# A rational activation behind an attention: a constant added by accumulating DMAs, Horner's form in more half units, and a new order of all steps

## The chip, the cores and the metric

One core of a Trainium2 chip runs the whole kernel in one launch. The metric is the device time in microseconds. A core has the engines TensorE (PE, with PEld for its weight loads), VectorE (DVE), ScalarE (ACT) and GpSimd (POOL), which run their own queues of instructions in order, and SyncE (SP), which here issues DMAs. Engines wait for each other through semaphores.

## The reference

Attention without a softmax, on features of degree two, and behind it one dense layer with a rational activation:

```python
def phi(x):                       # S1, S2: 8 x 32; 64 features
    a = einsum('rd,bhsd->bhsr', S1, x); b = einsum('rd,bhsd->bhsr', S2, x)
    return einsum('bhsi,bhsj->bhsij', a, b).reshape(..., 64)
kv = einsum('bhsf,bhsd->bhfd', phi(k), v);  z = phi(k).sum(axis=2)
x = (phi(q) @ kv) / (phi(q) @ z + 1e-6)     # 4 batches, 4 heads, 1088 tokens, 32 wide
h = x.reshape(4352, 128) @ w_in             # to 2048 wide
P = a[0] + a[1]*h + a[2]*h**2 + a[3]*h**3
Q = 1 + abs(b[0])*abs(h) + abs(b[1])*h**2
out = (P / (Q + 1e-6)) @ w_out              # 4352 x 128
```

## The kernel before

The 4352 tokens go through the dense layer in tiles: one of 256, seven of 512, and two of 256 at the end. With the 2048 rows of h on top, the work is cut into 17 *units* of 4096 columns by 128 partitions, each with two *half units* of 2048 columns; half unit n belongs to unit n // 2. A tile of 512 tokens has two units, one of 256 has one. The last unit is done partly in quarters.

One step of a unit is a word with a number and the unit behind the colon: `m1:5` is step m, part 1, of unit 5. A step that is done for both halves at once ("wide") is done at part 1.

- `h` (PE): four matrix products in f32 that make 1024 columns of h in PSUM. `e` (ACT): copies them to `hh` in bf16.
- `u` (DVE): |h|, by masking the sign. `ln` (ACT): the square that makes Q but for a factor and a constant. `ex` (ACT): the reciprocal of its root. The square of that, `r` = 1/Q, is made by `rd` on DVE, or by `ra` on ACT where `R_ON_ACT` has a 1.
- `pd` (DVE; `pa` on ACT for the last): p = a3*h + a2.
- `s` (DVE): s = h*r.
- `m` (DVE): the first product g. `x` (DVE): the second one, in place.
- `G` (PE): adds w_out times r, s and g to the tile's output in PSUM. There are three scaled copies of w_out (a0, a1 and 1 times a common factor), so that the output is a0*r + a1*s + g.
- `st`: DVE transposes a finished tile into `out_sb`, SP (at the end ACT too) stores it.

A half unit has one of two forms. In the plain form m makes g = h*s and x makes g = g*p; then r, s and g are multiplied by their copies of w_out, twelve matmuls where the tile has 512 tokens. In *Horner's form* m makes g = h*p, a step `v` adds a1 (a `tensor_scalar` on DVE over 128x2048), x makes g = g*s, and only r and g are multiplied: the four matmuls with s are left out. The tuple `HORNER` names the half units in that form. `WIDE_S`, `WIDE_M`, `WIDE_X` and `WIDE_P` name the units whose step is one instruction over 4096 columns, `SPLIT_A` those whose u is done by halves. r, s and g stand in rings of four half units, p in one of two.

The attention is in steps for keys (`kt`, `ks`, `kc`, `kf`, `kp`, `kk`) and for thirteen blocks of queries (`qt` transpose, `qs` sketch, `qc` copy, `qf` features, `qp` products, `qd`, `qi`, `qx` quotient, `qb` and `qk` back into xT). From block 3 on, qc sends the sketches to DRAM and reads them back spread over the partitions: SP issues four writes, then three reads, and qf on DVE waits for these. `lk`, `lq`, `lv`, `lw`, `lx` are loads on SP; k, q and v have one buffer each, so a load waits until the one before is used. `wo` scales w_out, `ba` makes |b| on ACT and the constants of Q on POOL, `bi` and `rg` finish them.

The order of all engines' queues is one hand-written list, `ORDER`; each engine takes its own steps from it in that order. So an engine waits whenever its next step isn't ready, and nothing overtakes.

At the end stands a branch: `special` is 1 if the constants b don't fit the fast form, and then the general kernel runs. The step `fl` loads the flag into a register on every engine; `hi` marks the branch's likely way.

Of the kernel before, what the change touches and what calls it, by code (L numbers as in the profile page):

```python
# [29 lines left out]
e1:1 h1:2 v1:0 u0:1 qf:3 qc:4 ln0:0 kc1:2 e3:1 ex0:0 kp1:1 qp:3 pd1:1 kf1:2 h3:2 ln0:1 s1:0 e1:2 rd0:0 qd:3 qi:3 G3:0  # L30
h0:2 ex0:1 e3:2 kk:1 e0:2 G0:0 x1:0 G5:0 qx:3 u1:1 qf:4 qs:5 qp:4 s0:0 u0:2 ln1:1 h2:2 lq:2 lk:3 qc:5 qd:4 qi:4 ex1:1
qt:7 qx:4 qb:3 qk:3 qb:4 lv:2 qk:4 x0:0 rd0:1 m1:1 ks0:2 qs:7 e2:2 u1:2 ln0:2 rd1:1 h2:3 v0:1 h0:3 e2:3 h1:3 v1:1
kc0:2 kf0:2 kt1:3 s1:1 ex0:2 qt:9 qf:5 e0:3 e1:3 kt0:3 ln1:2 G3:1 G2:0 h3:3 x1:1 h0:4 qc:7 e3:3 h3:4 ra0:2 st:0 qp:5
ex1:2 qd:5 qi:5 e0:4 ra1:2 kp1:2 s0:2 qx:5 G0:2 qs:6 u1:3 pd1:2 e3:4 qb:5 h1:4 qk:5 m0:2 G0:1 m1:2 h0:5 s1:2 qf:7
ln0:3 qc:6 e1:4 ln1:3 h2:4 x0:2 v1:2 G2:1 e0:5 ex1:3 qt:8 x1:2 pd1:3 h3:5 G1:2 kk:2 e2:4 ks0:3 ex0:3 qp:7 u1:4 e3:5
qs:8 ln0:4 rd0:3 rd1:3 h2:5 qd:7 e2:5 G3:2 qf:6 qc:8 s1:3 h1:5 G2:2 kc0:3 ln1:4 G5:1 kf0:3 qi:7 e1:5 lq:3 ex0:4 ex1:4
h1:6 G5:2 m1:3 h3:6 qx:7 u1:5 G3:3 ra0:4 qs:9 qp:6 x1:3 G0:3 rd1:4 G2:3 e1:6 ln0:5 st:2 pd1:4 lv:3 s1:4 h0:6 e3:6
ln1:5 qd:6 qi:6 qb:7 qf:8 G4:3 qx:6 qk:7 h2:6 m1:4 e0:6 qc:9 G0:4 ex1:5 qb:6 qk:6 qp:8 qt:10 ks1:3 h2:7 e2:6 G3:4
ex0:5 u1:6 x1:4 e2:7 h0:7 qd:8 ln1:6 G5:3 rd1:5 qi:8 h3:7 G1:4 G5:4 qt:12 G1:3 e0:7 G2:4 pd1:5 rd0:5 ex1:6 e3:7 h1:7
m1:5 kc1:3 ra1:6 qf:9 ln0:6 qx:8 e1:7 qp:9 qs:10 ex0:6 v0:5 qd:9 h1:8 s1:5 G4:4 u1:7 pd1:6 qc:10 h3:8 e1:8 st:4 qt:11  # L40
v1:5 rd0:6 qi:9 qb:8 G3:5 ln0:7 kf1:3 e3:8 ln1:7 h0:8 h2:8 x1:5 qk:8 qs:11 e0:8 ex1:7 kp1:3 s1:6 qx:9 G0:5 e2:8 G5:5
ex0:7 h2:9 kk:3 qf:10 h3:9 u1:8 qb:9 ra0:7 m0:6 G0:6 ra1:7 qs:12 m1:6 qc:11 x0:6 ln0:8 v1:6 e3:9 pd1:7 e2:9 qp:10 qk:9
qd:10 s1:7 G2:5 ln1:8 x1:6 G3:6 h0:9 qi:10 e0:9 h1:9 m1:7 ex0:8 qx:10 e1:9 pd1:8 v1:7 h1:10 u1:9 e1:10 rd0:8 ex1:8
rd1:8 G0:7 h0:10 G2:6 ln1:9 G3:7 e0:10 G1:6 ex1:9 qb:10 v0:7 h2:10 qk:10 e2:10 h3:10 s1:8 G5:6 qf:11 qp:11 ln0:9 h3:11
rd1:9 e3:10 h0:11 qd:11 ex0:9 m1:8 qi:11 e3:11 e0:11 u1:10 G3:8 G4:8 h2:11 x1:7 h1:11 x0:7 G2:7 ln1:10 qc:12 rd0:9
ln0:10 x1:8 e2:11 e1:11 G0:8 s1:9 ex1:10 ex0:10 G5:7 G1:8 h1:12 qx:11 qb:11 ra1:10 pd1:9 h0:12 qk:11 m1:9 u1:11 G0:9
x1:9 e1:12 G2:8 e0:12 h3:12 h2:12 rd0:10 qf:12 ln1:11 ln0:11 G5:9 G5:8 G1:9 s1:10 e2:12 G3:9 qp:12 ex0:11 pd1:10 e3:12
G0:10 ex1:11 m1:10 u1:12 rd0:11 h2:13 G3:10 ln1:12 ln0:12 e2:13 h3:13 qd:12 e3:13 G4:9 G2:9 rd1:11 h1:13 ex0:12 x1:10
h0:13 st:6 e1:13 s1:11 u1:13 ex1:12 pd1:11 m1:11 e0:13 G3:11 rd0:12 h2:14 ln1:13 h3:14 e2:14 G2:10 u0:13 ln0:13 G4:10
e3:14 qi:12 G1:11 x1:11 G1:10 rd1:12 qx:12 h1:14 ex1:13 st:8 s1:12 pd1:12 ex0:13 h0:14 e1:14 G0:11 qb:12 e0:14 ra0:13  # L50
rd1:13 G1:12 G5:10 G5:11 G4:11 qk:12 G3:12 h0:15 u1:14 ln0:14 m1:12 ln1:14 st:10 h1:15 x1:12 G0:12 G2:11 e0:15 h3:15
G4:12 ex1:14 e1:15 h2:15 s1:13 ex0:14 G3:13 pd1:13 m0:13 u0:15 G5:12 rd1:14 m1:13 e3:15 ln0:15 h1:16 e2:15 G4:13 G0:13
ex0:15 rd0:14 h0:16 G2:12 u1:15 ln1:15 e1:16 h2:16 G1:13 ex1:15 e0:16 x1:13 s1:14 ra0:15 G5:13 pd1:14 st:12 G2:13
G1:14 h3:16 m1:14 u0:16 x1:14 ra1:15 ln0:16 e2:16 ex0:16 e3:16 s1:15 u2:16 m1:15 G0:14 u3:16 G5:14 G1:15 G0:15 G3:14
# [66 lines left out]


def run(
# [525 lines left out]
    @skip()  # L649
    def d_v(i, h, hh):  # L650
        if horner(i, h):
            g = part_of(i, "g", h)
            nc.vector.tensor_scalar(out=g, in0=g, scalar1=a1, scalar2=None, op0=AX.add)
# [27 lines left out]
    def store(i):  # L681
        t0, tl, f0, per = units[i]
        if f0 + per < nf:
            return
# [1 line left out]
        nc.vector.transpose(out=o[:, :tl], in_=outs[t0][:, :tl])  # L686
# [106 lines left out]
    def flag():
        value.append(nc.values_load(special[0:1, :], min_val=0, max_val=1, skip_runtime_bounds_check_because="a comparison gives 0 or 1"))
# [9 lines left out]
    for step in plan.ORDER:  # L804
        name, i = step.split(":")
        i = int(i)
        if name in q_does:
            getattr(blocks[i](), q_does[name])()
        elif name in k_does:
            getattr(keys[i](), k_does[name][0])(*k_does[name][1:])  # L810
        elif name == "wo":
            w_part(i)
        elif name in loads:
            fetched[name, i] = loads[name](i)
        elif name == "tn":
            turn(i)
        elif name == "ba":
            nc.scalar.activation(out=b_abs, in_=b_sb, func=ACT.Abs)
# [49 lines left out]
```

## Time and profile before

| | us |
|---|---|
| median of three runs | 251.97 (251.5 to 252.45) |
| the profiled execution, its own time | 251.9 |
| its span, from the first to the last instruction | 250.0 |
| busy: PE, DVE, ACT, POOL | 240.5, 233.0, 227.9, 7.5 |
| HBM read and written | 16.16 MB and 3.15 MB |

The profile is of one execution. A *group* is all instructions of one line, engine, operation and shape; its row gives the count, then busy time, the mean duration in ns, and the idle time of the engine just before them with what ended it. L647 is line 647 of the listing. Instructions of one engine overlap by a little, so that a duration is somewhat more than what an instruction takes of the queue. TensorE's granted clock is 0.998 in the mean over the span.

### The profile page before, as it was taken

What the parts mean: (1) busy time and instruction counts of PE and PEld (TensorE: products, weight loads), DVE (VectorE), ACT (ScalarE), POOL (GpSimd) and SP (SyncE); (2) the same over time, 40 slices, a digit from 0 to 9 for tenths busy, and PEclk for the clock granted to TensorE, in tenths of its full rate; (3) what the DMA queues carried; (4) which work ended last, traced back from release to release, by engine and by line L of the source; (5) the groups of instructions that cost most, each with busy time, mean ns of one, the idle gap of its engine ahead of it and who ended that gap; (6) DMA issues with size and microseconds to landing.
All of it is one profiled execution on the core that took longest, in us unless ns stands there. A gap on an engine that the chain in (4) does not pass through costs nothing.

```text
span 250.0 us, 4083 instructions
## 1 busy us (share of the span) xinstructions
PE 240.5 (96%) x1585; PEld 133.8 (54%) x1585; DVE 233.0 (93%) x233; ACT 227.9 (91%) x217; POOL 7.5 (3%) x43
## 2 busy tenths in 40 slices
...
GB/s 155 257 387 89 99 121 188 134 156 78 144 27 100 28 202 138 69 45 16 148 22 77 67 3 0 16 102 3 0 42 0 40 25 22 0 37 8 0 49 42
DMA packets 30534, 19.60 MB, mean 78 GB/s; under 512 B 20400, under 2 KB 26672, under 8 KB 30512
## 3 DMA queue, kind: packets, MB, share of 16 engines
...
q8 instruction: 13, 0.21, 0.4%
q14 instruction: 9, 0.07, 0.1%
HBM read 16.16 MB, written 3.15 MB: 77 GB/s over the span
## 4 chain that ended last, share of the span: by engine, by line
PE 77%; DVE 13%; DMA 3%; issue 3%; SPq 0%; DVEq 0%
PE h_ps L519 42%; PE att_ps L677 23%; PE att_ps L428 4%; DVE g L658 4%; PE att_ps L364 4%; DVE g L647 3%; DVE s L643 2%; DMA k_sb<-in_k_dram 2%; PE att_ps L455 2%; DMA v_sb<-in_v_dram 2%; PE att_ps L473 2%; PE att_ps L323 1%; DVE p L600 1%; DVE r L630 1%; DVE out_sb L686 1%
## 5 line engine op out<-in xcount | busy, mean ns | idle before, releaser
L519 PE MATMUL h_ps<-xT,w_in_sb 128*128 128x512 f32 (+1 forms) x320 | 125.8, 532 | 0.0
L519 PEld LDWEIGHTS h_ps<-xT,w_in_sb 128*128 128x128 f32 x320 | 59.3, 190 | 44.4 <-issue 34.0
L525 ACT CAST hh<-h_ps 128x1024 bf16<-128x1024 f32 x68 | 72.2, 1086 | 2.1 <-PE h_ps L519 1.9
L613 ACT ACTIVATE ln<-u 128x2048 f32<-128x2048 bf16 (+1 forms) x35 | 67.2, 1950 | 0.0
L677 PEld LDWEIGHTS <-w_out 128*128 128x128 bf16 x432 | 41.8, 98 | 46.0 <-issue 16.5
L618 ACT ACTIVATE r<-ln 128x2048 bf16<-128x2048 f32 x22 | 44.0, 2002 | 0.0
L643 DVE TENSOR_TENSOR s<-hh,r 128x4096 bf16<-128x4096 bf16 (+2 forms) x21 | 39.2, 1872 | 0.0
L677 PE MATMUL att_ps<-r,w_out 128*128 128x512 bf16 (+1 forms) x160 | 34.8, 347 | 0.1
L677 PE MATMUL att_ps<-g,w_out 128*128 128x512 bf16 (+1 forms) x160 | 34.4, 347 | 0.0
L647 DVE TENSOR_TENSOR g<-hh,s 128x4096 bf16<-128x4096 bf16 (+2 forms) x16 | 27.8, 1744 | 0.3 <-PE att_ps L677 0.3
L658 DVE TENSOR_TENSOR g<-g,p 128x4096 bf16<-128x4096 bf16 (+2 forms) x15 | 27.7, 1849 | 0.0
L630 DVE TENSOR_TENSOR r<-r 128x2048 bf16<-128x2048 bf16 x22 | 26.5, 1217 | 0.0
L677 PE MATMUL att_ps<-s,w_out 128*128 128x512 bf16 (+1 forms) x112 | 24.5, 349 | 0.4 <-DVE s L643 0.4
L618 ACT ACTIVATE ln<-ln 128x2048 f32<-128x2048 f32 (+1 forms) x13 | 24.4, 1895 | 0.0
L624 ACT ACTIVATE r<-ln 128x2048 bf16<-128x2048 f32 (+1 forms) x13 | 23.7, 1868 | 0.0
L600 DVE TENSOR_SCALAR p<-hh,a_sb 128x4096 bf16<-128x4096 bf16 (+1 forms) x17 | 21.6, 1273 | 0.6 <-ACT hh L525 0.6
L548 DVE TENSOR_SCALAR u<-hh 128x2048 uint16<-128x2048 uint16 (+2 forms) x24 | 21.7, 905 | 0.4 <-ACT hh L525 0.4
L647 DVE TENSOR_TENSOR g<-hh,p 128x2048 bf16<-128x2048 bf16 (+1 forms) x7 | 11.6, 1663 | 0.0
L658 DVE TENSOR_TENSOR g<-g,s 128x2048 bf16<-128x2048 bf16 (+1 forms) x8 | 11.6, 1463 | 0.0
L428 PEld LDWEIGHTS att_ps<-kvz,q_pT 128*64 128x64 f32 x288 | 9.8, 137 | 3.3 <-issue 1.7
L428 PE MATMUL att_ps<-kvz,q_pT 128*64 128x66 f32 x288 | 11.1, 224 | 0.0
L364 PE MATMUL att_ps<-v_sb,k_p 128*64 128x64 f32 (+1 forms) x288 | 9.2, 222 | 1.0 <-DMA v_sb<-in_v_dram 1.0
...
## 6 DMA issues: line engine op xcount, KB each, us to landing
...
```

The costliest lines, as they stand in the source:

```text
L428: nc.tensor.matmul(self.nd[g * 64:(g + 1) * 64, o:o + 2 * KW], lhsT=self.q_p[:, c, x + g * 64:x + (g + 1) * 64], rhs=kvz[self.b % 2][:, c, ...
L519: nc.tensor.matmul(t[:, x * tl:(x + 1) * tl], lhsT=w_in_sb[:, f * 128:(f + 1) * 128], rhs=xT[:, x_at(t0):x_at(t0) + tl], start=True, stop= ...
L525: nc.scalar.copy(out=live[i]["hh"][:, part * PW:(part + 1) * PW], in_=live[i]["h", part])
L600: nc.vector.tensor_scalar(out=part_of(i, "p", h), in0=hh, scalar1=a3, scalar2=a2, op0=AX.mult, op1=AX.add)
L613: nc.scalar.activation(out=t, in_=live[i]["u"][:, span(h)], func=ACT.Square, scale=k_in_reg, bias=1.0)
L618: nc.scalar.activation(out=t if r_on_act(i, h) else part_of(i, "r", h), in_=t, func=ACT.Abs_reciprocal_sqrt, scale=k_sq_reg, bias=1.0)
L624: nc.scalar.activation(out=part_of(i, "r", h), in_=live[i]["ln", h], func=ACT.Square)
L630: nc.vector.tensor_mul(out=t, in0=t, in1=t)
L643: nc.vector.tensor_mul(out=part_of(i, "s", h), in0=hh, in1=part_of(i, "r", h))
L647: nc.vector.tensor_mul(out=part_of(i, "g", h), in0=hh, in1=part_of(i, "p" if horner(i, first(h)) else "s", h))
L658: nc.vector.tensor_mul(out=g, in0=g, in1=part_of(i, "s" if horner(i, first(h)) else "p", h))
L677: nc.tensor.matmul(outs[t0][:, :tl], lhsT=w_sb[y][:, f0 + x, :], rhs=part_of(i, key, h)[:, c:c + tl], start=done[0] == 0, stop=done[0] == ...
```

## The change

- `HORNER` has 25 half units instead of 10: 0 to 19, 22, and 24 to 27.
- In those, a1 is no longer added on DVE. A row `a1_row` (128x2048, bf16, every element a1) is made once by ACT, behind |b| in step `ba`; `v` is now a DMA issued by POOL that adds this row onto g in SBUF. x waits for it.
- `R_ON_ACT` loses half units 5 and 21, whose square goes to DVE. `SPLIT_A` is (0, 2, 3, 13, 16), `WIDE_S` gains unit 2, `WIDE_M` loses 1 and 11 and gains 2, 6 and 13, `WIDE_X` loses 4, 11 and 15 and gains 2, 6 and 7.
- The flag: `fl` loads it on SP, ACT and POOL only. A new last step `fm` copies, on POOL, first an element of the last output tile and then the flag into `late_special`, and PE and DVE load it from there.
- All steps stand in a new order. The dependences stay as they are. Among other things block 3's sketch (qs:3) comes ahead of block 2's, ln1:0 ahead of e1:0, lk:2 behind qc:3, and lv:3 behind st:4.

```diff
-    R_ON_ACT = (0, 0, 0, 0, 1, 1, 0, 0, 1, 0, 0, 0, 0, 1, 1, 1, 0, 0, 0, 0, 0, 1, 0, 0, 0, 0, 1, 0, 0, 0, 1, 1, 1, 1)
+    R_ON_ACT = (0, 0, 0, 0, 1, 0, 0, 0, 1, 0, 0, 0, 0, 1, 1, 1, 0, 0, 0, 0, 0, 0, 0, 0, 0, 0, 1, 0, 0, 0, 1, 1, 1, 1)
     ORDER = """
...
-kc2:0 qt:1 kf2:0 qc:0 kp0:0 ba:0 kp1:0 qf:0 kp2:0 qt:3 qs:1 kk:0 bi:0 qt:2 lq:1 lv:1 qc:1 qf:1 qp:0 qd:0 qs:2 qi:0
-qx:0 qb:0 wo:3 qc:2 qk:0 qf:2 wo:0 qp:1 qs:3 qp:2 qd:1 wo:5 wo:1 h2:0 qd:2 wo:4 e2:0 qi:1 h3:0 qx:1 qi:2 h0:0 wo:2
-qx:2 qb:1 rg:0 kt0:1 e3:0 e0:0 qb:2 pd1:0 qk:2 h1:0 kt1:1 u1:0 m1:0 lk:2 qk:1 e1:0 qc:3 ks0:1 ks1:1 qt:6 qt:4 h2:1
-pd0:0 u0:0 kc0:1 kc1:1 kf0:1 m0:0 kt0:2 ln1:0 h0:1 e2:1 kt1:2 ex1:0 e0:1 v0:0 rd1:0 h1:1 ks1:2 qs:4 kf1:1 h3:1 qt:5
+kc2:0 qt:1 kf2:0 qc:0 kp0:0 ba:0 kp1:0 qf:0 kp2:0 qt:3 qs:1 kk:0 bi:0 qt:2 lq:1 qc:1 qf:1 qp:0 qs:3 qs:2 qd:0 qi:0
+qx:0 qc:2 qb:0 qk:0 qp:1 lv:1 qf:2 wo:5 qd:1 wo:2 qi:1 qp:2 qc:3 wo:1 h2:0 qd:2 qx:1 wo:3 h3:0 rg:0 qb:1 wo:4 qi:2
+e2:0 qx:2 qb:2 wo:0 e3:0 h0:0 kt1:1 qk:1 kt0:1 ks1:1 qk:2 pd1:0 e0:0 ks0:1 kc1:1 u1:0 m1:0 v1:0 ln1:0 h1:0 kc0:1 kf1:1
+e1:0 h1:1 ex1:0 h2:1 kf0:1 e1:1 u0:0 pd0:0 qt:4 m0:0 rd1:0 qs:4 h0:1 e2:1 ln0:0 qt:6 s1:0 qf:3 lk:2 qc:4 e0:1 h3:1
+v0:0 x1:0 kp1:1 qp:3 h0:2 e3:1 u1:1 ex0:0 kk:1 kt0:2 qd:3 qt:5 kt1:2 ln1:1 ln0:1 G3:0 qi:3 pd1:1 e0:2 qx:3 qs:5 ks1:2
...
+h3:8 m1:5 e0:7 qf:9 kf0:3 qi:8 qc:10 x0:4 h2:8 ra1:6 v0:5 e3:8 e2:8 u1:7 ln0:7 G2:4 h1:8 rd0:6 pd1:6 qs:11 qp:9 e1:8
+ex0:7 qx:8 G0:5 st:4 h0:8 qb:8 ln1:7 v1:5 qk:8 m1:6 ex1:7 qd:9 x1:5 v1:6 lv:3 s1:6 G3:5 G0:6 qf:10 e0:8 u1:8 h3:9 e3:9
...
-G4:15 G5:15 pa2:16 pa3:16 s2:16 G6:16 hi:0 m3:16 G1:16 G4:16 G2:15 m2:16 G3:16 G7:16 x0:16 st:15 G2:16 x2:16 G5:16
-x3:16 G8:16 fl:0 st:16
+pa0:16 s3:16 s2:16 m3:16 G7:16 hi:0 pa2:16 G1:16 m2:16 x0:16 pa3:16 G1:15 G3:16 st:15 G4:16 x2:16 G2:16 G5:16 x3:16
+G8:16 fl:0 st:16 fm:0
     """.split()
-    SPLIT_A = (0, 1, 2, 13, 15, 16)
+    SPLIT_A = (0, 2, 3, 13, 16)
-    WIDE_S = (1, 3, 4, 5, 6, 7, 8, 9, 10, 11, 12, 13, 14, 15)
-    WIDE_M = (1, 3, 4, 5, 7, 8, 9, 10, 11, 12, 14, 15)
-    WIDE_X = (1, 3, 4, 5, 8, 9, 10, 11, 12, 13, 14, 15)
+    WIDE_S = (1, 2, 3, 4, 5, 6, 7, 8, 9, 10, 11, 12, 13, 14, 15)
+    WIDE_M = (2, 3, 4, 5, 6, 7, 8, 9, 10, 12, 13, 14, 15)
+    WIDE_X = (1, 2, 3, 5, 6, 7, 8, 9, 10, 12, 13, 14)
-    HORNER = (0, 1, 2, 3, 5, 10, 11, 13, 14, 15)
+    HORNER = (0, 1, 2, 3, 4, 5, 6, 7, 8, 9, 10, 11, 12, 13, 14, 15, 16, 17, 18, 19, 22, 24, 25, 26, 27)
...
+    a1_row = big.tile([128, 2048], BF, name="a1_row") if fast else None
+    late_special = consts.tile([1, 1], mybir.dt.int32, name="late_special")
...
     def d_v(i, h, hh):
         if horner(i, h):
             g = part_of(i, "g", h)
-            nc.vector.tensor_scalar(out=g, in0=g, scalar1=a1, scalar2=None, op0=AX.add)
+            if fast:
+                nc.gpsimd.dma_start(out=g, in_=a1_row, accum_op=AX.add)
+            else:
+                nc.vector.tensor_scalar(out=g, in0=g, scalar1=a1, scalar2=None, op0=AX.add)
...
         o = mid.tile([128, TC], FP, name="out_sb")
+        last_out[:] = [o]
...
     def flag():
-        value.append(nc.values_load(special[0:1, :], min_val=0, max_val=1, skip_runtime_bounds_check_because="a comparison gives 0 or 1"))
+        for e in (nc.sync, nc.scalar, nc.gpsimd):
+            e.reg_load(special_regs[e.engine], special[0:1, :])
+
+    def late_flag():
+        nc.gpsimd.tensor_copy(out=late_special, in_=last_out[0][0:1, 0:1])
+        nc.gpsimd.tensor_copy(out=late_special, in_=special[0:1, :])
+        for e in (nc.tensor, nc.vector):
+            e.reg_load(special_regs[e.engine], late_special)
+        value.append(nc.snap(special_handles, min_val=0, max_val=1))
...
             if fast:
                 fitting()
+                nc.scalar.activation(out=a1_row.rearrange("p (c x) -> p c x", c=4), in_=idle[:, None, :].to_broadcast([128, 4, 512]),
+                                     func=ACT.Identity, bias=a1, scale=1.0)
```

More of the change, by code (lines that the diff above doesn't have):

```diff
@@ L30 @@
[L30 to L54, printed above, removed]
@@ new lines @@
+e1:0 h1:1 ex1:0 h2:1 kf0:1 e1:1 u0:0 pd0:0 qt:4 m0:0 rd1:0 qs:4 h0:1 e2:1 ln0:0 qt:6 s1:0 qf:3 lk:2 qc:4 e0:1 h3:1
+v0:0 x1:0 kp1:1 qp:3 h0:2 e3:1 u1:1 ex0:0 kk:1 kt0:2 qd:3 qt:5 kt1:2 ln1:1 ln0:1 G3:0 qi:3 pd1:1 e0:2 qx:3 qs:5 ks1:2
+rd0:0 h2:2 m1:1 ex0:1 qb:3 s0:0 h1:2 kc1:2 qk:3 qf:4 m0:1 lk:3 ks0:2 lq:2 kt0:3 qc:5 qp:4 e2:2 e1:2 lv:2 h3:2 qd:4
+qi:4 u0:2 ex1:1 qx:4 v0:1 G5:0 qt:7 rd1:1 kc0:2 e3:2 u1:2 pd1:2 qb:4 kf1:2 G0:0 qk:4 ln0:2 kf0:2 rd0:1 h0:3 h1:3 x0:0
+ln1:2 e0:3 v1:1 qs:6 e1:3 qs:7 u0:3 h2:3 ex1:2 G3:1 G0:1 s1:1 qf:5 x1:1 qc:7 qt:9 h3:3 e2:3 G2:0 m1:2 ex0:2 ln0:3 qp:5
@@ new lines @@
+st:0 e3:3 ra0:2 rd1:2 qd:5 h0:4 qi:5 u1:3 qx:5 G5:1 e0:4 h1:4 qf:7 h3:4 ex0:3 e1:4 G3:2 pd1:3 qb:5 ln1:3 h2:4 qt:8
+s1:2 e3:4 qc:6 kp1:2 qk:5 v0:2 v1:2 e2:4 ex1:3 kk:2 u1:4 h0:5 rd0:3 rd1:3 ln1:4 kt1:3 x1:2 h1:5 e0:5 G2:1 G0:2 m1:3
+qp:7 ln0:4 h3:5 qf:6 e1:5 ex0:4 h2:5 e3:5 ex1:4 qs:8 lq:3 pd1:4 qp:6 s1:3 G5:2 v0:3 qd:6 G2:2 h2:6 qi:6 qc:8 qd:7
+qt:10 e2:5 qx:6 u1:5 qi:7 ra0:4 h3:6 rd1:4 ks0:3 ks1:3 qx:7 st:2 e2:6 m1:4 qb:6 ln0:5 v1:3 e3:6 s1:4 kc1:3 qb:7 ln1:5
+qk:7 h1:6 e1:6 x1:3 qk:6 h0:6 e0:6 qf:8 G3:3 qs:9 qt:11 G0:3 kc0:3 ex1:5 u1:6 h2:7 v0:4 ex0:5 pd1:5 qc:9 G0:4 rd0:5
@@ new lines @@
+ln0:9 e3:10 rd1:8 v1:7 qp:11 m1:8 G0:7 qb:9 qk:9 h0:10 qx:10 G3:7 ex0:9 e0:10 x1:7 qb:10 h2:10 qk:10 ln1:9 qd:11 G5:7
+e2:10 h2:11 v0:8 s1:8 G0:8 ex1:9 G2:7 rd0:9 e2:11 qi:11 u1:10 pd1:9 h3:11 h1:11 qf:12 ln0:10 rd1:9 qx:11 ln1:10 G3:8
+m1:9 e1:11 qp:12 qb:11 s1:9 v1:8 h0:11 e3:11 qk:11 ex0:10 e0:11 x1:8 v1:9 ex1:10 G0:9 h2:12 h0:12 u1:11 e2:12 rd0:10
+v0:9 G2:8 G0:10 rd1:10 ln0:11 h3:12 e0:12 pd1:10 ln1:11 e3:12 G3:9 s1:10 G5:8 ex1:11 h1:12 qd:12 G3:10 x1:9 h0:13
+e1:12 m1:10 ex0:11 G4:10 u1:12 h1:13 rd1:11 e0:13 ln1:12 rd0:11 h2:13 G2:9 e1:13 qi:12 ex1:12 G5:9 e2:13 x1:10 s1:11
```

19 lines of the change are left out of this document (15 added, 4 removed).

## The prediction

> **What bounds the kernel now.** I read the first part of the page, then the busy time by stretches, the groups by shape, and the timeline of one stretch, to see what an instruction costs when the next waits behind it.
>
> ```profile
> span 250.0 us, 4083 instructions
> PE 240.5 (96%) x1585; PEld 133.8 (54%) x1585; DVE 233.0 (93%) x233; ACT 227.9 (91%) x217; POOL 7.5 (3%) x43
> ```
> ```profile
> 0.00:30.00 30.00, 26.87 (x279) 18.29 (x280) 20.68 (x43) 15.75 (x30) 7.46 (x43) 1.00 0.72 205
> 60.00:220.00 160.00, 159.97 (x904) 82.11 (x903) 159.23 (x135) 159.89 (x140) 0.00 (x0) 1.00 0.22 53
> 220.00:240.00 20.00, 19.57 (x122) 13.22 (x121) 20.00 (x18) 20.00 (x16) 0.00 (x0) 1.00 0.17 25
> 240.00:250.00 10.00, 4.09 (x35) 3.06 (x32) 3.90 (x7) 2.65 (x3) 0.00 (x0) 0.96 0.23 34
> ```
> The columns are the stretch, its length, then busy us of PE, PEld, DVE, ACT, POOL, the granted clock, the DMA share and GB/s. From 60 to 220 us PE, DVE and ACT all stand still for less than 1 us out of 160, at a clock of 1.00. Three engines bound the kernel together: taking work from one gains nothing until the other two give as much. POOL is free, and the DMA engines are 0.22 busy.
>
> Busy time overlaps between neighbours, so I price by the distance from one start to the next:
>
> ```profile
> 215.62 2.29 DVE L658 TENSOR_TENSOR g<-g,p 128x4096 bf16<-128x4096 bf16 x1
> 217.82 2.28 DVE L643 TENSOR_TENSOR s<-hh,r 128x4096 bf16<-128x4096 bf16 x1
> 216.56 2.01 ACT L613 ACTIVATE ln<-u 128x2048 f32<-128x2048 bf16 x1
> 218.37 1.10 ACT L525 CAST hh<-h_ps 128x1024 bf16<-128x1024 f32 x1
> ```
> On DVE 2.29 us of duration take 2.20 of the queue: 0.08 less, in round numbers. On ACT 2.01 take 1.81: 0.2 less. For PE the chain of waits in order of time gives it directly:
>
> ```profile
> 80.94 0.86 PE att_ps L677 x4
> ```
> Four output matmuls of 512 columns take 0.86 us, so one is 0.215.
>
> **The change, part by part.**
>
> ```profile
> L630 DVE TENSOR_TENSOR r<-r 128x2048 bf16<-128x2048 bf16 x22 | 26.5, 1217 | 0.0
> L624 ACT ACTIVATE r<-ln 128x2048 bf16<-128x2048 f32 x11 | 21.6, 1995 | 0.0
> L677 PE MATMUL att_ps<-s,w_out 128*128 128x512 bf16 x80 | 20.2, 379 | 0.0
> L600 DVE TENSOR_SCALAR p<-hh,a_sb 128x4096 bf16<-128x4096 bf16 x15 | 20.0, 1334 | 0.0
> L548 DVE TENSOR_SCALAR u<-hh 128x4096 uint16<-128x4096 uint16 x11 | 13.4, 1214 | 0.4 <-ACT hh L525 0.4
> L653 DVE TENSOR_SCALAR g<-g,a_sb 128x2048 bf16<-128x2048 bf16 x10 | 7.2, 732 | 0.0
> L647 DVE TENSOR_TENSOR g<-hh,p 128x4096 bf16<-128x4096 bf16 x3 | 6.8, 2261 | 0.0
> L605 ACT ACTIVATE p<-hh,a_sb 128x2048 bf16<-128x2048 bf16 x1 | 2.1, 2112 | 0.0
> ```
> *Horner in 25 half units instead of 10.* A half unit in Horner form leaves out its matmuls with s. The 15 new ones all have tiles of 512 columns, four matmuls each: 60 x 0.215 = 12.9 us off PE. The multiplications on DVE stay as many.
>
> *The addition of a1.* DVE loses its ten of L653: 10 x 0.65 = 6.5 us. POOL issues 25 DMAs instead.
>
> *The square of r.* Half units 5 and 21 go from ACT to DVE: ACT loses 2 x 1.81 = 3.6 us, DVE gains 2 x 1.14 = 2.3 us.
>
> *Widths.* One unit more each for u, s and the first g in one instruction of 4096 instead of two of 2048 saves a start of about 0.07 us: 0.2 us off DVE. The second g keeps its counts.
>
> *The row of a1 (new, on ACT).* 128x2048 bf16; the nearest row is L605, 2.11 us, 1.9 of the queue. It stands behind b_abs, where ACT waits anyway:
>
> ```profile
> 9.74 0.21 ACT L818 ACTIVATE b_abs<-b_sb 128x2 f32<-128x2 f32 x1
> 12.55 0.54 ACT L374 COPY kvz<-att_ps 64x33 f32<-64x33 f32 x4 [2.60 <-PE att_ps L364]
> 21.74 1.01 ACT L525 CAST hh<-h_ps 128x1024 bf16<-128x1024 f32 x1 [0.61 <-PE h_ps L519]
> 23.47 1.01 ACT L525 CAST hh<-h_ps 128x1024 bf16<-128x1024 f32 x1 [0.71 <-PE h_ps L519]
> 25.64 1.01 ACT L525 CAST hh<-h_ps 128x1024 bf16<-128x1024 f32 x1 [0.60 <-PE h_ps L519]
> ```
> The hole of 2.60 us covers it; without that cover it would cost 1.9. The three holes after 20 us are ACT waiting for the first tiles of h. In the new order ln1:0 stands ahead of e1:0, so work of 1.81 us lies in front of the third: I take 0.6 us off ACT there and leave the other two (1.3 us) as the lower end.
>
> *The accumulating DMAs, waited for by x.* No row shows one. What covers each is the DVE work that the new order puts between m (writes g) and x (multiplies it). Unit 5 is the tightest pair: from m1:5 to x1:5 DVE has qf:9, kf0:3, qi:8, x0:4, u1:7, rd0:6, pd1:6, qx:8, st:4 and m1:6.
>
> ```profile
> L658 DVE TENSOR_TENSOR g<-g,s 128x2048 bf16<-128x2048 bf16 x6 | 7.1, 1198 | 0.0
> L496 DVE TENSOR_TENSOR q_pT<-a_all,b_all 128x640 f32<-128x640 f32 x4 | 3.3, 818 | 0.0
> L449 DVE TENSOR_TENSOR x_tok<-att_ps,rec 128x384 f32<-128x384 f32 x10 | 5.4, 544 | 0.0
> L686 DVE STREAM_TRANSPOSE out_sb<-att_ps 128x512 f32<-128x512 f32 x7 | 5.0, 709 | 0.0
> L335 DVE TENSOR_TENSOR k_p<-att_ps,b_sk 128x1024 f32<-128x1024 f32 x3 | 3.7, 1218 | 0.0
> L444 DVE RECIPROCAL rec<-den 128x12 f32<-128x12 f32 x10 | 2.2, 216 | 0.0
> ```
> Each less 0.08: 0.74 + 1.14 + 0.14 + 1.12 + 1.13 + 1.14 + 1.25 + 0.46 + 0.63 + 2.18 = 9.9 us. In the same way: units 2, 3 and 4: 11.1, 13.2, 10.3; 6 to 9: 10.4, 13.8, 15.3, 11.3; 12 and 13: 10.1, 12.5; unit 1: 14; the single half unit 11: 6.3; unit 0: 8.9 and more. In a pair, two DMAs of 512 KB must land one behind the other. Bounds for that:
>
> ```profile
> 10.00:20.00 10.00, 8.92 (x151) 7.50 (x152) 6.38 (x16) 5.09 (x11) 4.54 (x19) 1.00 1.08 349
> 1.59 4.42 DMA k_sb<-in_k_dram
> k_sb<-in_k_dram SPq DMA_DIRECT2D x1, 240.0 KB
> SPq L487 <- DMA sk_d<-sk_sb: 12.7, 17, 2.9
> ```
> At 349 GB/s, what the core moved when its DMA engines were full, 512 KB take 1.5 us. An accumulation reads its target too, so I count it twice: 3.0 us each. For what does not depend on size I take the longest wait for a small transfer to land, 2.9 us. A pair then needs 2.9 + 2 x 3.0 = 8.9 us, 1.0 inside the tightest cover: nothing on the path. The bad end is the 4.42 us in which 240 KB landed among other loads: 9.4 us for each 512 KB by size, and x would wait in nearly every unit. I am nearer the good end, since only 0.22 of the DMA time is taken in the long stretch. The Trainium skill, page "DMA: Bandwidth & Descriptors", section "Anatomy of one DMA — SWDGE (gpsimd) path", gives a DMA issued from GpSimd 2.0 us and its bytes at 436 GB/s: 3.2 us for one by that estimate, which says nothing of an accumulation. Behind a waiting DMA on POOL stand only later accumulations and the late flag; all that waits for them is x, and behind x DVE's queue.
>
> *The queue of SP.* lk:2 now stands behind block 3's round trip through DRAM and lv:3 behind st:4. Between the transposes that free k_sb (kt0:1) and kt0:2 the new order has 13.7 us of DVE work, and the load of 4.42 us fits: nothing. The round trips of the query sketches share the DMA engines with 13 MB of accumulations. One was late already:
>
> ```profile
> DVE q_pT L496 <- DMA b_all<-sk_d: 0.8, 1, 0.8
> ```
> I take no change and keep 0 to 2 us (two or three such waits).
>
> *The late flag.* DVE and PE read the flag only after the last output tile and two copies on POOL.
>
> ```profile
> 244.14 0.45 DVE L686 STREAM_TRANSPOSE out_sb<-att_ps 128x256 f32<-128x256 f32 x1 [0.69 <-PE att_ps L677]
> L794 DVEq TENSOR_LOAD <-special x1: 636/636/636, 242.7 to 242.7; - x1
> L836 SPq COMPARE_BRANCH  x1: 70/70/70, 247.2 to 247.2; - x1
> L772 POOL COPY c_fit<-b_fit 128x1 f32<-128x1 f32 x1 | 0.2, 183 | 0.0
> ```
> 244.6 + 2 x 0.18 + 0.64 is 245.6, and SP, with its output DMAs, branches only at 247.2: hidden, with 1.6 us to spare. If handovers eat more than that the cost is a few tenths. Nothing is gained either: the old load at 242.7 stood beside running work.
>
> **The sum.** PE -12.9. DVE -6.5 + 2.3 - 0.2 = -4.4. ACT -3.6 - 0.6 = -4.2. The smallest of the three counts: ACT and DVE become the bound together, and PE gets nearly 9 us of holes. The profiled execution took 251.9 us (0.07 under the median of the three runs, 251.97): 251.9 - 4.2 = **247.7 us**. Its own range is 245.8 (the other holes at the head go, and some of the end) to 250.5 (late round trips and flag).
>
> **Rivals.**
>
> *A. The accumulations are too slow.* If a pair needs 12.0 us (4.55 per DMA beside the 2.9), x waits: 0.9 in unit 2, 1.7 in 4, 2.1 in 5, 1.6 in 6, 0.7 in 9, 1.9 in 12, 1.1 in 11: 10.0 us, all on DVE, which has no slack: 251.9 - 4.2 + 10.0 = 257.7. It decides from a pair of about 11.1 us on, where the waits worked out so sum to 4.3. For it: nothing in the trace shows an accumulation, and the margin is 1.0 us. Against it: DMA shares of 0.1 to 0.5 in these stretches. Chance 0.18.
>
> *B. POOL and DVE get in each other's way.* If each of the 25 issues holds up DVE for as long as a small POOL instruction (L772, 0.18 us), DVE loses 25 x 0.18 = 4.6 us, and the time is 252.3. The trace has POOL at work only before 16 us, so it shows neither. The Trainium skill, page "SBUF — State Buffer", section "Who interferes with whom", speaks for it: VectorE in its two-port modes (a tensor_scalar in bf16 can be one) and GpSimd take a shared port pair from each other for a whole instruction, and descriptors written by GpSimd are starved meanwhile. No run here shows that. In this kernel L600 and L548 would be such instructions, 1.33 and 1.21 us. An issue put off by 1.33 us lengthens the pair to 10.2, 0.3 over unit 5's cover, which is nearly nothing; the loss would be on DVE. Chance 0.10.
>
> *C. PE alone sets the pace,* and ACT and DVE are full only because they are spread out: then all 12.9 us come through, 239.0. Against it: starts on both follow at the distance of their instruction, with no hole. Chance 0.03.
>
> **How the numbers follow.** Forecast 0.69, A 0.18, B 0.10, C 0.03. A measurement of this kernel can tell some 0.5%, 1.3 us. Faster: forecast and C, 0.72. Same: B, 0.10. Slower: A, 0.18. The range reaches from 245.5, just under the forecast's own, to A's 257.7; left out are C and the worse half of A, and some tails, under 0.2.
>
> **What would show it.** Right: PE busy drops to about 228 us and shows holes in the long stretch, waiting for ACT's hh; ACT and DVE stay full there; x waits for no DMA, and the last out_sb starts near 240 us. A: rows of DVE g waiting for a DMA on g, several us in sum, in units 4, 5, 6 and 12. B: tensor_scalars on DVE (L600, L548) get longer than 1.33 and 1.21 us beside POOL's issues. C: holes on ACT and DVE. Wrong in any case: an end that moves by over 2 us through the late flag.

## The result, and the profile after

| | before | after |
|---|---|---|
| median, us | 251.69 (251.31 to 252.45, 6 runs) | 260.21 (258.7 to 263.62, 6 runs) |
| ratio, with its 95% interval | | 1.0335 (1.0299 to 1.037) |
| profiled execution, us; its span | 251.9; 250.0 | 260.07; 258.2 |
| busy: PE, DVE, ACT, POOL | 240.5, 233.0, 227.9, 7.5 | 233.3, 228.8, 227.4, 31.1 |

The change makes the kernel 3.4% slower: 8.5 us more, where the prediction had 4.2 us less. (The ratio leaves out the run of 263.62 us, which is over 1.5% above the fastest.)

The page of after: busy time, then TensorE's granted clock and the DMA engines' busy share in 40 slices of 6.5 us, then the DMA queues (packets, MB, share of 16 engines):

```profile
PE 233.3 (90%) x1525; PEld 130.5 (51%) x1525; DVE 228.8 (89%) x222; ACT 227.4 (88%) x216; POOL 31.1 (12%) x70
...
PEclk9999999999999999999996899999999999997998
DMA  5994967698495459537798629352002381710052
...
q1 hardware_dynamic: 28864, 18.92, 28.3%
q0 software_dynamic: 3600, 13.11, 26.7%
```

DVE lost the work that was worked out (233.0 to 228.8 us), yet it ends later. The new queue q0 holds the accumulations, and they nearly double what the DMA engines have to do (26.7% of their time beside the 28.3% of q1). The same shows by stretches, first after, then the one row of before for 120 to 140 us:

```profile
60.00:220.00 160.00, 150.77 (x837) 77.56 (x836) 148.61 (x120) 149.94 (x134) 19.55 (x21) 0.98 0.55 118
120.00:140.00 20.00, 16.14 (x107) 8.66 (x107) 20.00 (x16) 18.89 (x16) 3.50 (x4) 0.94 0.90 191
140.00:160.00 20.00, 20.00 (x145) 10.99 (x142) 14.77 (x13) 14.47 (x17) 1.75 (x2) 0.89 0.62 145
```
```profile
120.00:140.00 20.00, 19.97 (x155) 10.53 (x154) 20.00 (x19) 19.92 (x19) 0.00 (x0) 1.00 0.38 95
```

In the long stretch DVE and ACT now stand still for 10 to 11 us out of 160, the DMA share goes from 0.22 to 0.55, and around 130 us it is 0.90. What the engines wait for in after, by its waits (us in total, times, longest; the second row is SP's own, which waits for a trip's writes before it issues the reads), and by a row of its groups and one of its DMA issues (KB each, median us from issue to landing):

```profile
DVE q_pT L498 <- DMA b_all<-sk_d: 11.3, 4, 4.7
```
```profile
SPq L489 <- DMA sk_d<-sk_sb: 22.7, 16, 2.8
```
```profile
L663 DVE TENSOR_TENSOR g<-g,s 128x4096 bf16<-128x4096 bf16 (+1 forms) x15 | 28.7, 1916 | 0.5 <-DMA g<-a_row 0.5
...
g<-a_row POOLq DMA_DIRECT2D x25, 512.0 KB, 6.4
```

x waits for an accumulation once in the whole run, for 0.5 us: each lands 6.4 us after its issue (median), within the cover. It is the attention's round trips through DRAM that are late: before they held up DVE for 0.8 us in all, and SP for 12.7 us. (The timeline has five waits of q_pT, 12.2 us in sum; for one of them, 0.9 us, the waits view names nothing.) One stretch, from the timeline (start and length in us, engine and line, what is done; in brackets how long the engine stood before, and for what):

```profile
125.16 5.47 SPq L700 DMA_DIRECT2D out_dram<-out_sb  x8
...
126.75 1.75 POOL L656 DMA_DIRECT2D g<-a_row  x2 [8.12 <-DVE g L649]
...
130.73 3.83 SPq L187 DMA_DIRECT2D v_sb<-in_v_dram  x4
...
137.01 1.75 POOL L656 DMA_DIRECT2D g<-a_row  x2 [8.51 <-DVE rec L446]
138.32 4.11 PE L366 MATMUL att_ps<-v_sb,k_p 128*64 128x64 f32 x72 [3.79 <-DMA v_sb<-in_v_dram]
...
139.64 2.16 SPq L492 DMA_DIRECT2D b_all<-sk_d  x2
...
148.79 0.96 DVE L498 TENSOR_TENSOR q_pT<-a_all,b_all 128x768 f32<-128x768 f32 x1 [4.74 <-DMA b_all<-sk_d]
```

The load of v (lv:3) goes out only after the eight stores of st:4, and beside a pair of accumulations; PE stands for 3.79 us. Within that wait, from 137.4 us on, its clock is halved for 6.8 us (the 6 and the 8 in the PEclk line), so what PE owes comes out late as well. The round trip behind v meets the next pair of accumulations, and DVE stands for 4.74 us.

### The profile page after: what moved, and what is told of

Its sections match the earlier page's. It is cut to its first block, busy times and chain, and to the rows that moved or that the text cites. A ratio compares the mean times of both kernels' runs of the same rounds, so it can differ in the third digit from the quotient of the medians.

```text
span 258.2 us, 4014 instructions
## 1 busy us (share of the span) xinstructions
PE 233.3 (90%) x1525; PEld 130.5 (51%) x1525; DVE 228.8 (89%) x222; ACT 227.4 (88%) x216; POOL 31.1 (12%) x70
## 3 DMA queue, kind: packets, MB, share of 16 engines
q1 hardware_dynamic: 28864, 18.92, 28.3%
q0 software_dynamic: 3600, 13.11, 26.7%
## 4 chain that ended last, share of the span: by engine, by line
PE 29%; DMA 21%; ACT 20%; DVE 14%; issue 7%; SPq 5%; POOL 1%; ACTq 0%; DVEq 0%; POOLq 0%
PE h_ps L521 14%; DMA b_all<-sk_d 13%; PE att_ps L682 9%; ACT ln L615 6%; ACT hh L527 5%; DMA g<-a_row 3%; ACT ln L620 3%; ACT r L626 2%; DVE u L550 2%; ACT r L620 2%; DVE g L663 2%; DVE p L602 2%; DVE s L645 2%; PE att_ps L366 2%; DMA v_sb<-in_v_dram 2%
## 5 line engine op out<-in xcount | busy, mean ns | idle before, releaser
L527 ACT CAST hh<-h_ps 128x1024 bf16<-128x1024 f32 x68 | 69.6, 1039 | 2.2 <-PE h_ps L521 1.6
L682 PEld LDWEIGHTS <-w_out 128*128 128x128 bf16 x372 | 36.5, 99 | 47.8 <-issue 25.5
L656 POOL DMA_DIRECT2D g<-a_row x25 | 23.2, 1095 | 180.3 <-DVE g L649 146.0
L663 DVE TENSOR_TENSOR g<-g,s 128x4096 bf16<-128x4096 bf16 (+1 forms) x15 | 28.7, 1916 | 0.5 <-DMA g<-a_row 0.5
L649 DVE TENSOR_TENSOR g<-hh,p 128x4096 bf16<-128x4096 bf16 (+1 forms) x15 | 28.7, 1916 | 0.0
L602 DVE TENSOR_SCALAR p<-hh,a_sb 128x4096 bf16<-128x4096 bf16 (+1 forms) x17 | 21.6, 1273 | 0.7 <-ACT hh L527 0.7
L550 DVE TENSOR_SCALAR u<-hh 128x4096 uint16<-128x4096 uint16 (+2 forms) x23 | 21.5, 940 | 0.7 <-ACT hh L527 0.7
L498 DVE TENSOR_TENSOR q_pT<-a_all,b_all 128x768 f32<-128x768 f32 (+1 forms) x10 | 9.0, 901 | 12.2 <-DMA b_all<-sk_d 11.3
L620 ACT ACTIVATE ln<-ln 128x2048 f32<-128x2048 f32 (+1 forms) x11 | 19.4, 1792 | 0.0
L626 ACT ACTIVATE r<-ln 128x2048 bf16<-128x2048 f32 (+1 forms) x11 | 19.3, 1795 | 0.0
L366 PEld LDWEIGHTS att_ps<-v_sb,k_p 128*64 128x64 f32 (+1 forms) x288 | 10.5, 160 | 7.4 <-issue 5.8
```

The source lines that it names most:

```text
L366: nc.tensor.matmul(out.rearrange("p (n d) -> p n d", d=D), lhsT=self.k_p[part][:sl, t - self.PARTS[part][0], 2 * c + a].rearrange("p i j - ...
L527: nc.scalar.copy(out=live[i]["hh"][:, part * PW:(part + 1) * PW], in_=live[i]["h", part])
L550: nc.vector.tensor_scalar(out=t[:, c].bitcast(U16), in0=live[i]["hh"][:, c].bitcast(U16), scalar1=0x7FFF, scalar2=None, op0=AX.bitwise_and)
L602: nc.vector.tensor_scalar(out=part_of(i, "p", h), in0=hh, scalar1=a3, scalar2=a2, op0=AX.mult, op1=AX.add)
L620: nc.scalar.activation(out=t if r_on_act(i, h) else part_of(i, "r", h), in_=t, func=ACT.Abs_reciprocal_sqrt, scale=k_sq_reg, bias=1.0)
L649: nc.vector.tensor_mul(out=part_of(i, "g", h), in0=hh, in1=part_of(i, "p" if horner(i, first(h)) else "s", h))
```

## The experiments

Two theories for the 8.5 us. *Crowding*: the accumulations take time of the DMA engines, and the small packets of the round trips, of k and of v, which stand on a critical chain, wait behind them. *Order*: the new list of steps puts things behind each other on SP's queue and elsewhere that were apart before, and would lose the time without any accumulation.

**The accumulations left out** (g lacks a1).

```diff
-                nc.gpsimd.dma_start(out=g, in_=a1_row, accum_op=AX.add)
+                pass
```


> The changed kernel with its 25 accumulating DMAs left out (a1 is not added in those half units); order, widths and late flag stay. Crowding theory (the accumulations' 4096-byte packets, 328 ns each on every DMA engine, hold up the small packets of SP's loads and of the sketches' round trips): the five waits of q_pT for b_all, 12.2 us in sum, fall under 1.5 us, the wait for v_sb and the dip of the clock go, time 247 to 249.5. Order theory (the new order leaves the round trips and lv:3 too little distance, whatever else uses the DMA engines): waits over 6 us stay, time 254 or more.

Measured: 251.41 us (ratio to before 0.9964, 0.9933 to 0.9995). That lies between the theories. The accumulations cost 8.8 us here (260.2 to 251.4; PE's wait for v goes with them), but the order alone does not bring the 4.2 us either. The two long waits that are left stand at block 4, at 43 us, and at 136 us:

```profile
DVE q_pT L498 <- DMA b_all<-sk_d: 3.4, 2, 2.9
PE att_ps L430 <- DVE x_tok L451: 2.7, 1, 2.7
```

**The accumulations in pieces of 512 columns.**

```diff
-                nc.gpsimd.dma_start(out=g, in_=a1_row, accum_op=AX.add)
+                nc.gpsimd.dma_start(out=g.rearrange("p (c x) -> p c x", c=4), in_=a1_row[:, None, 0:512].to_broadcast([128, 4, 512]), accum_op=AX.add)
```


> The changed kernel with each accumulation cut into pieces of 512 elements (1024 bytes; the source is a quarter of the row, read four times): same bytes, four times the packets. Crowding by long packets: SP's small packets stand behind a quarter of the time per turn, q_pT's waits fall from 12.2 to under 5 us, time 251 to 255, while an accumulation may land later. If the bytes' time on the engines counts and not the packet's length: waits stay near 12 us, 259 to 262. Order theory: 259 to 262 too.

Measured: 259.18 us (ratio 1.0306, 1.0285 to 1.0326).

```profile
q0 software_dynamic: 13200, 13.11, 32.4%
```

The waits stay (q_pT 10.3 us), so shorter packets alone do not help. The pieces take a fifth more engine time, though (32.4% of 255.7 us against 26.7% of 258.2), so a small gain from the shorter packets may hide behind that.

**lv:3 back behind st:2**, where the load of v is out of the stores' way.

```diff
-... ks1:3 qx:7 st:2 e2:6 ...   ... v1:6 lv:3 s1:6 ...
+... ks1:3 qx:7 st:2 lv:3 e2:6 ...   ... v1:6 s1:6 ...
```


> The changed kernel with one step moved: lv:3 stands behind st:2 again, ahead of sk9, as in the kernel before. Crowding theory: only PE's wait for v_sb (3.8 us) and what follows it (half clock for 6.8 us, ACT waiting 5.5 us for PE) go, 254.5 to 257.5; q_pT's other waits stay. Order theory, with lv:3 as its main part: under 251.

Measured: 257.61 us (ratio 1.0264, 1.0217 to 1.031). The wait for v and the half clock at 137 us are gone; the round trips are still late (before the same step DVE stands for 3.2 us more, for which the view names nothing):

```profile
DVE q_pT L498 <- DMA b_all<-sk_d: 6.0, 4, 2.1
```

**The kernel before, with only its ten additions of a1 made accumulations.**

```diff
-            nc.vector.tensor_scalar(out=g, in0=g, scalar1=a1, scalar2=None, op0=AX.add)
+            nc.gpsimd.dma_start(out=g, in_=a1_row, accum_op=AX.add)
```


> The kernel before, its order and its ten Horner half units, with a1 added there by accumulating DMAs (row made by ACT behind b_abs); the flag as before. DVE loses 6.5 us of work, PE and ACT nothing, so without crowding PE holds the time at 250.5 to 252. Crowding theory: ten accumulations in units 0 to 7 meet the round trips of blocks 3 to 11, q_pT waits 2 to 6 us, time 252.5 to 256. Order theory: no such waits, 250.5 to 252.

Measured: 259.77 us (ratio 1.033, 1.0312 to 1.0347). In the old order ten accumulations alone cost 8 us, more than the crowding theory expected, though they take 6.5 us of work off DVE:

```profile
q0 software_dynamic: 1440, 5.24, 11.1%
```
```profile
DVE q_pT L497 <- DMA b_all<-sk_d: 5.7, 3, 3.3
DVE g L662 <- DMA g<-a_row: 4.9, 3, 2.3
PE att_ps L429 <- DVE q_pT L497: 3.6, 1, 3.6
```

Here x waits too, since that order was not made with a cover for it. PE's wait of 3.6 us again goes with half the clock, for 6.8 us, so round trips are not the whole of this cost.

**Both loads moved, no accumulations** (g lacks a1): as in the experiment on lv:3, and lk:2, which stands ahead of block 4's round trip, up behind kt0:1.

```diff
-... qk:1 kt0:1 ks1:1 ...   ... s1:0 qf:3 lk:2 qc:4 ...
+... qk:1 kt0:1 lk:2 ks1:1 ...   ... s1:0 qf:3 qc:4 ...
```


> Two loads moved in the new order: lv:3 back behind st:2, and lk:2 up behind kt0:1, so that it no longer stands directly ahead of block 4's round trip. The accumulations of a1 are left out (g lacks a1). If what was left to lose without the accumulations (251.4 us) is the 2.9 us q_pT wait at block 4 and the 2.3 to 2.7 us hole at 136 to 142 us, and both come from these two loads, 246 to 247 us, with no q_pT wait of over 1 us. If the waits belong to the order as a whole and only move, 250 to 251.4 us.

Measured: 247.34 us (ratio 0.9833, 0.9804 to 0.9862). That is 4.1 us less than with the loads where they were, and the long stretch is full again:

```profile
60.00:220.00 160.00, 156.21 (x875) 80.66 (x874) 159.18 (x128) 159.86 (x141) 0.00 (x0) 1.00 0.21 52
```

But only lv:3 has moved in a queue. Between the old and the new place of lk:2 in the list stands no other step of SP: its order is qc:3, lk:2, qc:4 either way. Block 4's wait still fell, from 2.9 to 0.6 us. SP's writes of that block and the first of its reads, without the accumulations, before the move and then after it:

```profile
32.78 1.84 SPq L486 DMA_DIRECT2D sk_d<-sk_sb  x4
...
38.23 0.55 SPq L489 DMA_DIRECT2D a_all<-sk_d  x1
```
```profile
33.36 1.78 SPq L486 DMA_DIRECT2D sk_d<-sk_sb  x4
...
36.44 0.55 SPq L489 DMA_DIRECT2D a_all<-sk_d  x1
```

The reads went out 3.6 us after the last write was issued in the one and 1.3 us in the other, after the same issues in the same order. The order does not explain this difference, and the runs do not show what does. So the hole at 136 us went with lv:3's move, and how much of the 4.1 us is lv:3's is open. (Ten runs without the move took 249.49 to 252.65 us; so at least 1.9 us lie between any of them and the slowest run here, 247.57.)

**Both loads moved, with all accumulations.** The same moves in the kernel after.

> The same two loads moved, with the accumulations as in the kernel after. If lk:2 was in block 4's way here too, its q_pT wait of 2.1 us goes: 255 to 255.8 us, against 257.6 with lv:3 moved alone. If the accumulations alone hold up block 4, 257 to 258 us and the wait stays. In both cases the difference to the same kernel without accumulations is what their traffic costs: by the crowding theory 7 to 9 us.

Measured: four runs from 255.44 to 262.02 us, and no ratio is given. As lk:2's move changes no queue, this is the kernel of the experiment on lv:3 once more: the traces of the two have the same instructions in the same order on every engine. So it says nothing of lk:2. It says that one and the same kernel took 257.18 to 259.69 us in four runs and 255.44 to 262.02 in four others, so that the gain by lv:3 beside accumulations is less sure than its ratio. The accumulations cost at least 8 us here too (255.4 against 247.3), and the waits of q_pT go on (5.3 us for b_all, and 5.5 for which the view names nothing).

**A plain copy in place of the accumulation** (both loads moved; the output lacks p*h in those half units).

```diff
-                nc.gpsimd.dma_start(out=g, in_=a1_row, accum_op=AX.add)
+                nc.gpsimd.dma_start(out=g, in_=a1_row)
```


> As with both loads moved, but each of the 25 DMAs copies a1_row over g instead of adding to it (the output is without p*h there): same issues, same waits, same bytes written; a 4096-byte packet is expected at about 0.16 us instead of 0.33. If the engine time of the accumulations crowds the round trips, about half of their cost goes, some 4 us faster than with accumulations, and q_pT waits of 3 to 5 us in sum instead of 9. If it is the number of DMAs and packets in the queues, no difference to the kernel with accumulations (within 1 us).

Measured: 249.28 us (ratio 0.9901, 0.9873 to 0.9928). The queue of the copies, then that of the accumulations with both loads moved:

```profile
q0 software_dynamic: 3600, 13.11, 13.8%
...
g<-a_row POOLq DMA_DIRECT2D x25, 512.0 KB, 3.8
```
```profile
q0 software_dynamic: 3600, 13.11, 26.2%
```

As many DMAs, packets and bytes written, at half the engine time: 2 us instead of 8 or more. So the number of DMAs is not it, nor their issue on POOL. What differs is the engine time, and that an accumulation also reads its target, which these runs do not separate; the cost grows faster than in proportion to the engine time. The engines' own work is no slower beside accumulations: DVE is busy for 228.8 us in the kernel after and for 228.6 without any.

**POOL adds a1 itself** (both loads moved).

```diff
-                nc.gpsimd.dma_start(out=g, in_=a1_row, accum_op=AX.add)
+                nc.gpsimd.tensor_scalar(out=g, in0=g, scalar1=a1, scalar2=None, op0=AX.add)
```


> As with both loads moved, but POOL itself adds a1 in SBUF (tensor_scalar, 25 times 128x2048 bf16), with no DMA. If POOL and DVE do not disturb each other, as fast as the kernel without accumulations, 246 to 249 us, since two such instructions of some 2 us each fit into the cover of 9.9 us. If they get in each other's way, DVE's instructions beside it become longer than 1.34 us (p, L602) and 1.22 us (u, L550), and DVE loses up to POOL's whole time, 25 times 1 to 2 us: 270 to 300 us.

Measured: 344.93 us (ratio 1.3713, 1.3674 to 1.3753), worse than expected; one addition on POOL takes 7.35 us instead of some 2. Three groups of this kernel, then the same ones without accumulations:

```profile
L656 POOL TENSOR_SCALAR g<-g,a_sb 128x2048 bf16<-128x2048 bf16 x25 | 183.5, 7350 | 112.5 <-DVE g L649 98.1
...
L602 DVE TENSOR_SCALAR p<-hh,a_sb 128x4096 bf16<-128x4096 bf16 (+1 forms) x17 | 53.9, 3170 | 0.7 <-ACT hh L527 0.7
L645 DVE TENSOR_TENSOR s<-hh,r 128x4096 bf16<-128x4096 bf16 (+2 forms) x20 | 44.9, 2247 | 0.0
```
```profile
L645 DVE TENSOR_TENSOR s<-hh,r 128x4096 bf16<-128x4096 bf16 (+2 forms) x20 | 39.0, 1956 | 0.0
...
L602 DVE TENSOR_SCALAR p<-hh,a_sb 128x4096 bf16<-128x4096 bf16 (+1 forms) x17 | 21.6, 1273 | 0.7 <-ACT hh L527 0.7
```

A `tensor_scalar` on DVE takes 3170 ns instead of 1273 in the mean beside POOL at work, a `tensor_tensor` 2247 instead of 1956. In all DVE is busy for 322.7 us instead of 228.6, nearly the whole of the 97.6 us that the kernel loses; x waits for POOL for only 5.3. For the `tensor_scalar` this fits what the Trainium skill says on its page "SBUF — State Buffer", section "Who interferes with whom": the port pair that VectorE's two-port modes share with GpSimd belongs to one of them for a whole instruction.

**The round trips started earlier**: two buffers for a_all and b_all, and qc right behind qs for eight blocks; both loads moved, all accumulations kept. The room comes from k_p, which has two buffers instead of three and borrows one of hh (not among the lines below).

```diff
-    PB, AB = 1, 1
+    PB, AB = 1, 2 if fast else 1
...
-... qs:4 h0:1 e2:1 ln0:0 qt:6 s1:0 qf:3 qc:4 ...
+... qs:4 qc:4 h0:1 e2:1 ln0:0 qt:6 s1:0 qf:3 ...
```


> Both loads moved, all 25 accumulations kept; a_all and b_all get two buffers each instead of one (room made by giving k_p two buffers, the third part of block 0 borrowing one of hh), and the copy and round trip of blocks 4, 5, 6 and 8 to 12 (qc) are issued right behind their sketches (qs), so that each starts 2 to 12 us earlier. If the accumulations cost time only by making the round trips late, the q_pT waits (10.7 us in sum with both loads moved) go but for 0 to 2 us, and the time is 248 to 250.5 us, near the 247.3 us without accumulations. If their traffic costs something else as well (k and v loads, x waiting for g, the half clock), or the trips are late however early they start, 253 us or more.

Measured: 287.31 us (ratio 1.1433, 1.1386 to 1.1479). A miss, and an instructive one: SP waits for each block's writes before it issues the reads, and the loads of the next k and q now stood behind that; DVE waited 10.5 us for k and 13.4 us for q. SP's part of the timeline, and the wait on DVE that follows from it:

```profile
45.94 1.22 SPq L493 DMA_DIRECT2D b_all<-sk_d  x2
47.26 0.39 SPq L174 DMA_DIRECT2D k_sb<-in_k_dram  x1
```
```profile
DVE kT L317 <- DMA k_sb<-in_k_dram: 11.9, 2, 10.5
```

**The same, with lq:2, lk:3 and lq:3 ahead of those round trips.**

```diff
-... kt0:2 qd:3 qt:5 kt1:2 ...   ... m0:1 lk:3 ks0:2 lq:2 kt0:3 ...
+... kt0:2 qd:3 qt:5 lq:2 kt1:2 lk:3 ...   ... m0:1 ks0:2 kt0:3 ...
```


> The kernel with two buffers for a_all and b_all and early round trips, but with the loads of q and k (lq:2, lk:3, lq:3) put ahead of the round trips that stood in front of them in SP's queue (287 us with them behind, where DVE waited 10.5 us for k and 13.4 us for q). If the accumulations cost time only by making the trips late, the early start now hides that: q_pT waits of 0 to 2 us in sum, 248 to 251 us. If the trips still hold up what is queued behind them on SP, or x and the loads wait for other reasons, 254 us or more.

Measured: 266.9 us (ratio 1.0618, 1.0588 to 1.0648). The loads are in time again, but the trips are not: one block's is late by 6.7 us.

```profile
55.53 6.29 SPq L487 DMA_DIRECT2D sk_d<-sk_sb  x4
64.50 0.55 SPq L490 DMA_DIRECT2D a_all<-sk_d  x1
```
```profile
DVE q_pT L499 <- DMA b_all<-sk_d: 10.1, 4, 6.7
```

From the first of four writes of some 24 KB to the reads SP is held for 9 us. Of the 6.29 us that the writes take to issue, SP waits 4.9 for reads of the trip before to land. A slow trip on SP delays the next one, so an earlier start doesn't hide it. That the accumulations could be kept by starting trips earlier was wrong in this form.

**The accumulations of units 9 to 13 alone** (both loads moved; seven of 25, the other g lack a1).

```diff
-                nc.gpsimd.dma_start(out=g, in_=a1_row, accum_op=AX.add)
+                if i >= 9:
+                    nc.gpsimd.dma_start(out=g, in_=a1_row, accum_op=AX.add)
```


> The kernel with both loads moved (247.3 us without accumulations), with the accumulations of units 9 to 13 alone (7 of 25; the g of the other half units lacks a1). They start late, where only the last round trip and the stores are left. If accumulations cost only what they do to round trips, 247.3 to 248.5 us, with no q_pT wait but perhaps one at block 12. If each costs some 0.3 us wherever it stands (10 us over 25, by the DMA engines, by SBUF or by GpSimd's work), 249.5 to 250.5 us.

Measured: 247.41 us (ratio 0.9834, 0.9813 to 0.9854), against 247.34 without any.

```profile
q0 software_dynamic: 1008, 3.67, 7.6%
```
```profile
DVE q_pT L498 <- DMA b_all<-sk_d: 0.7, 2, 0.6
```

The first of the seven is issued at 156.9 us, after the last round trip has been used (q_pT at 151.7 us). There accumulations cost nothing that these runs can tell, so all of the 8 us and more must come with the 18 in the attention's time.

**The old flag** (both loads moved, no accumulations, so g lacks a1).

```diff
-        for e in (nc.sync, nc.scalar, nc.gpsimd):
-            e.reg_load(special_regs[e.engine], special[0:1, :])
+        value.append(nc.values_load(special[0:1, :], min_val=0, max_val=1, skip_runtime_bounds_check_because="a comparison gives 0 or 1"))
```


> The kernel with both loads moved and no accumulations (g lacks a1; 247.3 us), with the flag loaded on all engines before the last store, as in the kernel before. By the prediction the late load is hidden: the same time, 247.1 to 247.6 us, and the same 6.6 us from the start of the last out_sb to the end of the span. By the tails of the profiles (6.6 us against 5.9 us before) it costs 0.5 to 0.8 us: 246.5 to 246.9 us, and a tail of 5.8 to 6.0 us.

Measured: 248.5 us (247.56 to 249.69). The last out_sb, with the late flag and with the old one:

```profile
239.09 0.45 DVE L692 STREAM_TRANSPOSE out_sb<-att_ps 128x256 f32<-128x256 f32 x1 [0.73 <-PE att_ps L682]
```
```profile
239.60 0.45 DVE L690 STREAM_TRANSPOSE out_sb<-att_ps 128x256 f32<-128x256 f32 x1 [0.69 <-PE att_ps L681]
```

The spans are 245.7 and 246.1 us, so the tails are 6.6 and 6.5 us: the late flag is hidden. The median is 1.2 us above that with the late flag, and above what either case expected, which the tail doesn't explain; the ratios to the kernel before (0.9879, 0.9833 to 0.9924, and 0.9833, 0.9804 to 0.9862) overlap. The old flag brings nothing.

## Why the prediction was wrong

*The sum was right, for a kernel that was not there.* PE, DVE and ACT as worked out gave 247.7 us. With lv:3 back in its place and no accumulations it is 247.34, with seven of them 247.41. DVE is busy for 228.6 us there, 4.4 less than before, as worked out; PE's 230.9 us are more than the 227.6 of the working, which costs nothing, as PE is not the bound. Of ACT's three holes at 21 to 25 us two are left (0.57 and 0.38 us), nearly as taken, and the row of a1 is hidden: the hole of 2.60 us shrinks to 0.91.

*The price of an accumulation was right.* 26.7% of a span of 258.2 us, over 25, is 2.76 us of all 16 engines, where the prediction counted 3.0. The cover held, and x waited 0.5 us, but not by the forecast's margin alone: unit 4's pair landed 10.4 us after the first issue, against a cover of 10.3, and was in time because DVE itself stood 2.77 us for b_all in between. So rival A, which has the sign right and whose 257.7 us is near, is not what happened. The estimate of 3.2 us from issue to landing, from the Trainium skill's page "DMA: Bandwidth & Descriptors", section "Anatomy of one DMA — SWDGE (gpsimd) path", is a little under what the plain copy took among other traffic (3.8 us), and half of the accumulation's 6.4.

*Rival B did not come either.* L602 takes 1273 ns beside accumulations and without them. POOL's 25 issues leave DVE alone, and its busy time with it (228.8 and 228.6 us, where the rival had 4.6 more); POOL's arithmetic doesn't.

*The step that failed* is the one on SP's queue: "I take no change and keep 0 to 2 us (two or three such waits)". It measured 11.3 us of waits for b_all by the waits view. Two things were wrong in it. The engine time was in the working (25 times 3.0 us is 75 us of all engines, on top of a share of 0.22) and was weighed only against x; nobody asked who else stands in line. The mean of 0.22 hid that the round trips come in busier moments: from 120 to 140 us the share was 0.38 before, and 0.90 after. The Trainium skill's page "DMA: Bandwidth & Descriptors", section "Issuing engines are not separate DMA queues", has the rule that was missing: DMAs of all issuers end on the same 16 engines and interleave there. The runs agree: POOL issued the accumulations, and the trips that SP issued were late by them.

*The same step, on lk:2 and lv:3.* "the load of 4.42 us fits: nothing" asked whether k is in time for its own reader. It is, though that row is of 240 KB and lk:2 moves 544: kT stands for no load of k there. Whether lk:2 ahead of block 4's round trip makes that late is not shown: the experiment that moved lk:2 left SP's queue as it was. For lv:3 behind st:4 the prediction named the move and no price; beside accumulations it was the 3.79 us of PE's wait, with half the clock, and 2.6 us of the whole (260.21 to 257.61), a size that the spread of the later runs of that same kernel (255.44 to 262.02) leaves uncertain. Without accumulations it is part or all of the 4.1 us.

*The late flag* is hidden, as taken: the tails differ by a tenth of a microsecond.

What stays open: how much of the 260.2 us the halved clock makes (with lv:3 back, where PE's long wait is gone and no such spell falls there, it is 2.6 us less, both effects together), what lk:2 would be worth ahead of block 3's round trip, where it stood before, and why block 4's writes landed so differently in two executions with the same order. No kernel here that computes the whole output beats the one before: a place for the 18 early additions of a1 that costs less than they do on DVE was not found.
